# A planned attention-and-MoE kernel: loads cut into smaller pieces that are issued at landings, and new constants in its planner

## The chip, the cores and the metric

The kernel runs on one core of one Trainium2 chip. The metric is device time in microseconds of one execution. Engines are named as in the profile: PE (matrix multiply), PEld (its weight loads), DVE, ACT, POOL and SP; POOL issues the input loads and SP the output stores.

## The reference

Sliding-window attention over 8 batches, 8 heads, 576 positions, head size 64; then a soft mixture of experts on its output. Heads 0 to 3 see the last 32 positions, heads 4 to 7 every fourth of the last 128.

```python
scores = scale * q @ k.T                     # per batch and head
mask_plain = (rel >= 0) & (rel < 32)
mask_dil   = (rel >= 0) & (rel < 128) & (rel % 4 == 0)
attn = softmax(where(mask, scores, -1e9));  x = attn @ v      # x: 4608 x 512
logits = x @ phi                             # 32 slots, 4 per expert
d = softmax over tokens;  slot_input = d.T @ x
h = relu(slot_input[e] @ w1[e]);  slot_out[e] = h @ w2[e]     # 8 experts, F = 1024
c = softmax over slots;  out = c @ slot_out  # 4608 x 512, f32
```

Inputs are f32: q, k and v of 9.4 MB each, w1 and w2 of 16.8 MB each. The output is 9.4 MB.

## The kernel before, in words

**A program of ops and a planner.** The kernel doesn't write instructions in their final order. `P.op` (L123) records an op: which engines could run it and for how long by the author's estimate (`pe(t)`, `act(n)`, `dve(n)`, `dve2(n)`, L304 to L317), which buffers it reads and writes, which PSUM banks it needs, how many matmuls it has (`mm`), and, for a load, its bytes and semaphore. `schedule` (L162) then simulates the ops by these durations and takes, again and again, the op that could start first, with priority among those that start within `SLACK` of it. The result is a fixed order of instructions for each engine, and for ops that DVE or ACT could run the choice of the engine. `emit` (L238) writes that order with the semaphore waits that each op needs. On the chip the engines run their orders as given: an op that isn't ready holds up all behind it on its engine.

**The work.** 16 units, one for each batch and half of the heads. A unit has these stages: `stage_T` (L615) transposes K, Q and V from staging slots (L623 for an even unit, 18 matmuls each; L626 for an odd one, 9 each); `stage_V` (L639, matmuls L655) lays V out in 18 blocks; `stage_S` (L670) adds mask and scores in PSUM (L678, L681, and 72 small matmuls at L687); `stage_P` (L697) takes the maximum on DVE (L706, L708), subtracts it by matmul (L715), takes the exponential on ACT (L721) and transposes (L728); `stage_O` (L737) multiplies by V in 72 small matmuls (L749) and normalises on DVE (L759, L761); `stage_X` (L765) transposes the result (L779). After each second unit `gating` (L793) does the logits (L803), the running softmax over tokens, transposes (L836 to L853) and the sum into the slots (L870 to L880); after each fourth `combine` (L892) prepares the softmax over slots (L899 to L924). After the last unit come the experts: w1 at L1024, transposes L1044, w2 at L1058, of which the last two groups are expert 7's chunks 0 to 5 and 6 to 7. Then 36 matmuls (L1082) with copies (L1090, L1091), and 18 stores of 512 KB (L1095).

**The loads.** All are DMAs that POOL issues, casting f32 to bf16. `load` (L467, issue at L477) brings K, Q or V of a unit as one DMA into one of 9 staging slots, three units ahead; an even unit's has 256 rows of 1,152 bytes at the destination, an odd unit's 128 rows of 2,304. A slot can be loaded again only after the transposes that read it. `load_w` (L480, issue at L492) brings an expert's w1 or w2 in two DMAs of 64 partitions each (expert 7's w2 in chunks 0 to 5 and 6 to 7). Stage loads have priority 100n-100 and weights 1700, so that in the plan a weight load goes only where no stage load can. The last two experts' w2 lie in staging slots.

**What paces a load.** All but the first unit's loads are `paced`. Before, the planner lets a paced load start no earlier than 2.5 us (`DMA_LEAD` + `DMA_WAIT`) before its model of the DMA queue is free, 400 bytes a nanosecond. On the chip this becomes a wait for the op of PE, DVE, ACT or SP whose planned end lies last before the load's planned start:

```python
            if o.paced:
                near = [d for d in done_at[-60:] if d.end <= st]
                if near:
                    o.raw = o.raw | {max(near, key=lambda d: d.end)}
```

**The planner's model of instruction blocks.** It counts the matmuls given to PE. An op that would carry the count over `BLOCK` (127) may not start before a time that is `SUPPLY` (3.2 us), less half of the op, after the start of the op at which the count went over last:

```python
                if o.opts[0][0] == "PE" and n_mm + o.mm > self.BLOCK:
                    t0 = max(t0, blk_t + self.SUPPLY - 0.5 * o.opts[0][1])
```

The delay exists in the plan only; no wait on the chip comes from it. Its effect is the order.

Of the kernel before, what the change touches and what calls it, by code (L numbers as in the profile page):

```python
# [13 lines left out]
DM = H * D  # L14
E_EXP = 8
N_SLOTS = 32
FF = 1024
SCALE = 1.0 / (D ** 0.5)
NSU = 16
LSEQ = 2 * S  # L20
# [88 lines left out]
class Prog:  # L109
    LAT = dict(PE=0.28, DVE=0.08, ACT=0.08, POOL=0.1, SP=0.1)  # L110
    SLACK = 0.12
    DVE_MORE = 0.5
    BLOCK = 127
    SUPPLY = 3.2
    DMA_LEAD = 2.2
    DMA_WAIT = 0.3

    def __init__(self):
        self.ops = []
# [42 lines left out]
    def schedule(self):  # L162
        free = dict(PE=0.0, DVE=0.0, ACT=0.0, POOL=0.0, SP=0.0)
        dma_free = 0.0
        n_mm, blk_t = 0, 0.0
        done_at = []
        for o in self.ops:
            o.users = []
        for o in self.ops:
            o.nleft = 0  # L170
            for d in o.raw | o.war:
                d.users.append(o)
                o.nleft += 1
        done = lambda d: d.end + (0.0 if d.bytes else self.LAT[d.eng])
        ready = []

        def arm(o):
            o.start = max([done(d) for d in o.raw | o.war], default=0.0)
            ready.append(o)
        for o in self.ops:  # L180
            if o.nleft == 0:
                arm(o)
        order = []
        while ready:
            cands = []
            for o in ready:
                t0 = o.start
                bank = None
                if o.rounds and o.rounds[0].first is None:
                    rd = o.rounds[0]  # L190
                    bank = rd.pool.choose(rd.n, t0, done)
                    if bank is None:
                        continue
                    t0 = max(t0, bank[0])

                if o.paced:
                    t0 = max(t0, dma_free - self.DMA_LEAD - self.DMA_WAIT)

                if o.opts[0][0] == "PE" and n_mm + o.mm > self.BLOCK:
                    t0 = max(t0, blk_t + self.SUPPLY - 0.5 * o.opts[0][1])  # L200
                e, c = min(o.opts, key=lambda ec: max(t0, free[ec[0]]) + ec[1] +
                           (o.more if ec[0] == "DVE" else 0.0))
                cands.append((max(t0, free[e]), o.prio, o.idx, o, e, c, bank))
            assert cands, "no schedule"
            first = min(cands, key=lambda x: x[:3])
            same = [x for x in cands if x[4] == first[4] and x[0] <= first[0] + self.SLACK]
            st, _, _, o, e, c, bank = min(same, key=lambda x: (x[1], x[2]))
            if bank is not None:
                rd = o.rounds[0]
                rd.first = bank[1]  # L210
                for i in range(rd.n):
                    rd.pool.banks[bank[1] + i].round = rd
                o.war = o.war | (set(bank[2]) - o.raw)
            o.eng, o.start, o.end = e, st, st + c
            free[e] = st + c
            if e == "PE":
                n_mm += o.mm
                if n_mm > self.BLOCK:
                    n_mm, blk_t = n_mm - self.BLOCK, st
            if o.paced:  # L220
                near = [d for d in done_at[-60:] if d.end <= st]
                if near:
                    o.raw = o.raw | {max(near, key=lambda d: d.end)}
            if not o.bytes and e != "POOL":
                done_at.append(o)
            if o.bytes:
                dma_free = max(dma_free, o.end + 1.5) + o.bytes / 400e3
                o.end = dma_free + 0.5
            order.append(o)
            ready.remove(o)  # L230
            for u in o.users:
                u.nleft -= 1
                if u.nleft == 0:
# [82 lines left out]
def pe(t):  # L316
    return [("PE", t)]  # L317
# [12 lines left out]
def bass_dilated_sliding_attn__then__soft_moe_slots_kernel(  # L330
# [11 lines left out]
    P = Prog()  # L342
# [5 lines left out]
    NSLOT = 9  # L348
# [5 lines left out]
    slots = [stg_all[:, SLOT * i:SLOT * (i + 1)] for i in range(NSLOT)]  # L354
# [30 lines left out]
    mm = sb("mm", [128, B + 1, 2], F32)  # L385
# [37 lines left out]
    b_stg = [Buf() for _ in range(NSLOT)]  # L423
# [23 lines left out]
    s_stg = [nc.alloc_semaphore(f"s_stg{i}") for i in range(NSLOT)]  # L447
    s_w1 = [nc.alloc_semaphore(f"s_w1_{e}") for e in range(E_EXP)]
    s_w2 = [nc.alloc_semaphore(f"s_w2_{e}") for e in range(E_EXP)]
    s_w2l = [s_w2[E_EXP - 1], nc.alloc_semaphore("s_w2_last")]  # L450
# [16 lines left out]
    def load(w):  # L467
        n, t = w // 3, w % 3
        b, ty = su_bt(n)
        i = w % NSLOT  # L470
        hs = (k, q, v)[t][b, 4 * ty:4 * ty + 4]
        if ty == 0:
            dst = slots[i].rearrange("p (h c) -> p h c", h=2)
            ap = hs.rearrange("(p x) (i c) d -> (x i) p (c d)", p=2, c=9)
        else:
            dst, ap = slots[i], hs.rearrange("h (i c) d -> (h i) (c d)", c=18)
        P.op(POOL, lambda g: g.dma_start(dst, ap),  # L477
             w=[b_stg[i]], dma=(128 * LSEQ * 5, s_stg[i]), paced=n > 0)

    def load_w(kk, e):  # L480
        src, c, dst, b_w, sem = ((moe_w1, 4, w1b[:, e], b_w1[e], s_w1[e]) if kk == "1" else
                                 (moe_w2, 8, w2v[e], b_w2[e], s_w2[e]))
        ap = src[e].rearrange("(p c) f -> p c f", c=c)
        for i in range(2):
            if kk == "2" and e == E_EXP - 1:

                sl = (slice(0, 128), slice(0, 6) if i == 0 else slice(6, 8))
                size, bw, sem = DM * FF * (3 - 2 * i), b_w2l[i], s_w2l[i]
            else:
                sl = (slice(64 * i, 64 * i + 64), slice(0, c))  # L490
                size, bw = DM * FF * 2, b_w
            P.op(POOL, lambda g, sl=sl: g.dma_start(dst[sl], ap[sl]), paced=True,  # L492
                 dma=(size, sem), **(dict(w=[bw]) if i == 0 or bw is not b_w else dict(a=[bw])))


    P.cur = -1000
# [118 lines left out]
    def stage_T(n):  # L615
        u = n % 2
# [11 lines left out]
        for t in range(3):  # L628
            rd = Round(ring, 2)
            i = (3 * n + t) % NSLOT  # L630
            o = P.op(pe(0.47), lambda pe_, rd=rd, i=i: trs(pe_, rd, slots[i]),
                     r=[b_stg[i], b_ident], rounds=[rd], mm=18 - 9 * u)
            o.war |= set(b_seq[u][t].w + b_seq[u][t].r)
            dv = seq[u][:, t, PAD:PAD + LSEQ].rearrange("p (m c) -> p m c", c=9)
            P.op([act(1152), dve(1152)], lambda eng, dv=dv, rd=rd: cp(
                eng, dv, rd.h[:, 0:1152].rearrange("p (c m) -> p m c", m=128)),
                rounds=[rd], w=[b_seq[u][t]])

    def stage_V(n):  # L639
# [8 lines left out]
        for gi, part in enumerate((todo[:16], todo[16:])):  # L648
# [7 lines left out]
                                            seq[u][:, 2, sl], ident[:])  # L656
                return ins
            nt = sum(len(w) for w in part)
            o = P.op(pe(0.055 * nt), tr, r=[b_seq[u][2], b_ident], rounds=[rd], mm=nt)
            if gi == 0:  # L660
                o.war |= set(b_VOV[u].w + b_VOV[u].r)
            n_el = 128 * len(part)
# [7 lines left out]
    def stage_S(n):  # L670
# [3 lines left out]
        for p, t0, nt in ((0, 0, 10), (1, 10, 8)):  # L674
            rd = Round(ring, 2 - p)

            def fS(pe_, p=p, t0=t0, nt=nt, rd=rd):
# [6 lines left out]
                for p_ in range(2):  # L684
# [4 lines left out]
                                qk(u, p_, k, j, 1, 32, 0), qk(u, p_, k, j, 0, 64, 1),  # L689
                                start=False, stop=True, skip_group_check=True)  # L690
                return ins
            P.op(pe(0.06 * nt), fS, mm=4 * nt + 2 - p, rounds=[rd],
                 r=rr + [b_mask[u], b_mb, b_ident])
            res.append((rd, t0, nt))
        return res
# [1 line left out]
    def stage_P(n, rds):  # L697
        u = n % 2
        for i, (rd, t0, nt) in enumerate(rds):
# [11 lines left out]
            def sub(pe_, rd=rd, nt=nt, hi=hi, lo=lo):  # L711
                for a, b in ((0, 8), (8, nt)):
# [3 lines left out]
                                             m[:, a:b].unsqueeze(2).to_broadcast([128, b - a, 64]),  # L716
                                             start=False, stop=True, skip_group_check=True)
                return ins
            P.op(pe(0.08 + 0.0006 * ne), sub, r=[b_nm[u][i], b_nl[u][i], b_idneg],
                 rounds=[rd], mm=4 - 2 * i)  # L720
            P.op([act(ne)], lambda ac, t0=t0, rd=rd, ne=ne: ac.activation(  # L721
                pb[u][:, 64 * t0:64 * t0 + ne], rd.f[:, 0:ne], ACTF.Exp, scale=SCALE),
# [2 lines left out]
        for i, (a, b) in enumerate(((0, 5), (5, 9))):  # L725
            def tr(pe_, a=a, b=b):
# [1 line left out]
                    ins = pe_.transpose(rd.h[:, 128 * t:128 * t + 128],  # L728
                                        pb[u][:, 128 * t:128 * t + 128], ident[:])
                return ins  # L730
            o = P.op(pe(0.05 * (b - a)), tr, r=[b_pb[u][i], b_ident], rounds=[rd], mm=b - a)
# [5 lines left out]
    def stage_O(n):  # L737
        u = n % 2
        x = n % NX
        for p in range(2):  # L740
# [5 lines left out]
            def fO(pe_, p=p, rd=rd):  # L746
# [46 lines left out]
    def gating(b):  # L793
# [6 lines left out]
        def fL(pe_):  # L800
# [6 lines left out]
        P.op(pe(0.4), fL, r=[b_phi, b_xt[xs[0]], b_xt[xs[1]]], rounds=[rl], mm=16)  # L807
# [47 lines left out]
        P.op(pe(0.25), fD1, r=[b_dT, b_dT2, b_ident], rounds=[rd], mm=5)  # L855
        P.op(pe(0.15), fD2, r=[b_dT, b_dT2, b_ident], rounds=[rd], mm=5, hard=[o0])
# [4 lines left out]
        def fSl(pe_):  # L861
# [3 lines left out]
            for ty in range(2):  # L865
# [7 lines left out]
                if ty == 0:  # L873
# [8 lines left out]
        P.op(pe(0.7), fSl, r=[b_dn, b_xn[xs[0]], b_xn[xs[1]]], rounds=[rs], mm=20)  # L882
        if b == B - 1:
            return rs
        P.op([("DVE", 0.75)], lambda vv: vv.scalar_tensor_tensor(
# [255 lines left out]
```

## Time and profile before

| what | us |
|---|---|
| three runs | 245.57, 247.24, 251.96 (median 247.24) |
| the profiled execution: its time | 246.26 |
| its span, first to last instruction | 244.5 |
| PE, PEld busy | 186.6, 127.9 |
| DVE, ACT, POOL busy | 144.9, 122.8, 53.2 |
| packets of the loads (queue q0), share of 16 engines' span | 74.7% |
| last load lands, from the span's start | 213.9 |
| last w2 matmul group ends, first output matmul starts | 217.1, 217.8 |

Lines of the profile name an engine, a source line, an operation, the tile written and the tile read. `[2.73 <-issue]` behind an instruction means that its engine stood idle 2.73 us before it and that no semaphore event ended this; any other name there is the op that ended the wait. The chain is the run of work that ended last, followed back from the end. The clock is the share of TensorE's full clock that was granted. Besides these views the trace has a record for each DMA packet: queue, start, duration and bytes.

### The profile page before, as it was taken

How to read it: one execution, taken by the hardware profiler on the slowest of the kernel's cores; microseconds unless marked ns; L12 is line 12 of the kernel's file. 1: busy time of each engine (PE TensorE's matmuls, PEld its weight loads, DVE VectorE, ACT ScalarE, POOL GpSimd, SP SyncE). 2: the span in 40 equal slices, each digit the busy share in tenths (PEclk: the TensorE clock that was granted, in tenths of full speed). 3: DMA queues.
4: the chain of work that ended last, by engine and by line, in shares of the span. 5: the costliest groups of instructions: out<-in, count | busy, mean ns of one | idle time of the engine just before them, and what ended most of it. 6: DMA issues, size and time to landing. Idle time of an engine off the chain costs nothing.

```text
span 244.5 us, 9798 instructions
## 1 busy us (share of the span) xinstructions
PE 186.6 (76%) x4502; PEld 127.9 (52%) x4502; DVE 144.9 (59%) x319; ACT 122.8 (50%) x190; POOL 53.2 (22%) x113
## 2 busy tenths in 40 slices
PE   0896959897987869897989777996688586987410
PEld 0585746675665557663767555765466352542100
DVE  4145456557778766863788655768277556627440
ACT  2546835576747727673656644765444320135440
POOL 6545321312312222320223111111011210000000
PEclk9999997889999999996799997999797855999955
DMA  6979794979899997797799998699689999609998
GB/s 84 147 121 137 118 163 78 132 119 155 142 185 153 162 172 136 126 159 144 127 160 137 191 154 155 127 181 174 127 150 176 201 182 167 127 5 406 401 407 328
DMA packets 15881, 41.06 MB, mean 168 GB/s; under 512 B 2144, under 2 KB 8288, under 8 KB 13920
## 3 DMA queue, kind: packets, MB, share of 16 engines
q0 software_dynamic: 12672, 30.94, 74.7%
q1 hardware_dynamic: 3168, 9.50, 10.0%
q8 instruction: 35, 0.57, 0.9%
q14 instruction: 6, 0.05, 0.1%
HBM read 61.93 MB, written 9.44 MB: 292 GB/s over the span
## 4 chain that ended last, share of the span: by engine, by line
PE 64%; DVE 11%; issue 10%; DMA 7%; ACT 4%; POOL 0%; DVEq 0%; POOLq 0%
PE ps L655 7%; PE ps L715 7%; PE ps L687 6%; PE ps L623 6%; PE ps L626 5%; DMA out_dram<-aren 5%; PE ps L728 4%; PE ps L779 4%; PE ps L678 3%; PE ps L749 3%; DVE aren L327 3%; DMA stg_all<-in_v_dram 3%; DVE xn L761 2%; PE ps L1082 2%; PE ps L1058 2%
## 5 line engine op out<-in xcount | busy, mean ns | idle before, releaser
L326 ACT ACTIVATE aren<-ps 128x1152 bf16<-128x1152 bf16 (+2 forms) x48 | 53.5, 1130 | 38.2 <-PE ps L655 17.8
L327 DVE COPY aren<-ps 128x1152 bf16<-128x1152 bf16 (+2 forms) x32 | 33.5, 1053 | 15.3 <-PE ps L655 6.4
L706 DVE TENSOR_REDUCE nm<-ps 128x10 f32<-128x640 f32 (+1 forms) x32 | 24.1, 754 | 14.8 <-PE ps L687 14.8
L687 PE MATMUL ps<-aren 64*32 64x64 bf16 x1152 | 17.3, 194 | 16.5 <-issue 16.5
L687 PEld LDWEIGHTS ps<-aren 64*32 64x32 bf16 x1152 | 12.0, 94 | 26.4 <-issue 26.4
L326 ACT ACTIVATE xt<-ps 128x640 bf16<-128x640 bf16 (+1 forms) x20 | 12.7, 659 | 25.5 <-PE ps L779 25.5
L761 DVE TENSOR_TENSOR xn<-ps,rv 128x576 bf16<-128x576 f32 x32 | 24.2, 758 | 1.1
L655 PE MATMUL ps<-ident,aren 128*128 128x128 bf16 (+1 forms) x304 | 23.5, 236 | 1.2 <-issue 0.5
L721 ACT ACTIVATE pp<-ps 128x640 bf16<-128x640 f32 (+1 forms) x32 | 20.4, 652 | 6.1 <-PE ps L715 5.4
L623 PE MATMUL ps<-ident,stg_all 128*64 128x128 bf16 x432 | 17.7, 235 | 7.0 <-DMA stg_all<-in_k_dram 6.2
L655 PEld LDWEIGHTS ps<-ident,aren 128*128 128x128 bf16 (+1 forms) x304 | 18.6, 107 | 3.4 <-issue 1.0
L623 PEld LDWEIGHTS ps<-ident,stg_all 128*64 128x64 bf16 x432 | 14.1, 119 | 10.7 <-POOL mbase L510 6.2
L1091 DVE COPY aren<-ps 128x512 f32<-128x512 f32 x18 | 11.9, 688 | 11.4 <-PE ps L1082 6.6
L626 PE MATMUL ps<-ident,stg_all 128*128 128x128 bf16 x216 | 18.1, 238 | 0.7 <-DVE aren L327 0.7
L715 PE MATMUL ps<-nm,idneg 128*128 128x512 bf16 (+1 forms) x48 | 16.9, 359 | 0.6 <-DVE nl L708 0.4
L749 PE MATMUL ps<-aren,pp 64*32 64x65 bf16 x1152 | 14.2, 195 | 3.7 <-issue 1.5
L492 POOL DMA_DIRECT2D w1b<-in_moe_w_dram x16 | 8.5, 529 | 38.1 <-PE ps L749 9.0
L626 PEld LDWEIGHTS ps<-ident,stg_all 128*128 128x128 bf16 x216 | 15.1, 108 | 3.0 <-DVE aren L327 0.9
L477 POOL DMA_DIRECT2D stg_all<-in_k_dram x16 | 10.3, 644 | 26.4 <-DVE nl L708 4.4
L715 PE MATMUL ps<-nl,idneg 128*128 128x512 bf16 (+1 forms) x48 | 15.4, 355 | 0.0
L728 PE MATMUL ps<-ident,pp 128*128 128x128 bf16 x144 | 13.8, 230 | 2.0 <-DVE nl L708 1.3
L477 POOL DMA_DIRECT2D stg_all<-in_v_dram x16 | 9.9, 619 | 23.3 <-DVE nl L708 4.6
(143 smaller groups left out, 302.8 us busy)
## 6 DMA issues: line engine op xcount, KB each, us to landing
out_dram<-aren SPq DMA_DIRECT2D x18, 512.0 KB, 5.5
w1b<-in_moe_w_dram POOLq DMA_DIRECT2D x16, 512.0 KB, 7.1
w2b<-in_moe_w_dram POOLq DMA_DIRECT2D x12, 512.0 KB, 7.2
stg_all<-in_k_dram POOLq DMA_DIRECT2D x16, 288.0 KB, 5.3
stg_all<-in_q_dram POOLq DMA_DIRECT2D x16, 288.0 KB, 5.3
stg_all<-in_v_dram POOLq DMA_DIRECT2D x16, 288.0 KB, 5.1
stg_all<-in_moe_w_dram POOLq DMA_DIRECT2D x2, 512.0 KB, 7.3
stg_all<-in_moe_w_dram POOLq DMA_DIRECT2D x1, 768.0 KB, 8.5
```

Source lines behind the costliest of these rows:

```text
L326: return eng.activation(dst, src, ACTF.Copy)
L327: return eng.tensor_copy(dst, src)
L623: ins = pe_.transpose(rd.h[64 * p:64 * p + 64, oc], sl[:, 576 * p + 64 * c:576 * p + 64 * c + 64], ident[:])
L626: ins = pe_.transpose(rd.h[:, oc], sl[:, oc], ident[:])
L655: ins = pe_.transpose(rd.h[row:row + nk, 128 * i:128 * i + 128], seq[u][:, 2, sl], ident[:])
L687: ins = pe_.matmul(rd.f[32 * j:32 * j + 32, 64 * (tile - t0):64 * (tile - t0) + 64], qk(u, p_, k, j, 1, 32, 0), qk(u, p_, k, j, 0, 64, 1), ...
L706: P.op([dve(ne)], lambda vv, sv=sv, nv=nv: vv.tensor_reduce(nv, sv(), AXX, AluOp.max), rounds=[rd], w=[b_nm[u][i]])
L715: ins = pe_.matmul(rd.f[:, 64 * a:64 * b], idneg[:], m[:, a:b].unsqueeze(2).to_broadcast([128, b - a, 64]), start=False, stop=True, skip_g ...
L721: P.op([act(ne)], lambda ac, t0=t0, rd=rd, ne=ne: ac.activation(pb[u][:, 64 * t0:64 * t0 + ne], rd.f[:, 0:ne], ACTF.Exp, scale=SCALE), rou ...
L728: ins = pe_.transpose(rd.h[:, 128 * t:128 * t + 128], pb[u][:, 128 * t:128 * t + 128], ident[:])
L749: ins = pe_.matmul(rd.f[32 * oq:32 * oq + 32, 103 * pl:103 * pl + 65], pt[u][sl, tile // 2, 32 * j:32 * j + 32], VOV[u][sl, pv, j % 2 if u ...
L761: P.op([dve(576)], lambda vv, cols=cols, rvp=rvp, p=p: vv.tensor_tensor(xn[x][:, :, p, :], cols(0, 64), rvp.unsqueeze(2).to_broadcast([128 ...
```

## The change

It does four things.

1. A stage load becomes two DMAs of 64 partitions each, and a weight load four of 32 (expert 7's w2: four of two chunks each), every one with a semaphore of its own. A reader waits for all pieces that it reads. 80 issues become 160.
2. A paced load no longer waits for a compute op. It waits for the landing of an earlier load: going back from the last load issued, the planner adds up planned transfer times (bytes over 400 a nanosecond) until they reach `COVER` (1.8 us), and takes the load before those. Its landing is the earliest start in the plan, and a wait on its semaphore on the chip.
3. The block model starts with the count at `BLOCK` - `FIRST` (127.3 - 94), so its places are 94, 221.3, 348.6 and so on in place of 127, 254, 381; `SUPPLY` is 3.4; the time of a place is taken inside the op, in proportion to its matmuls.
4. The estimated durations of 11 PE ops change, nearly all upwards. The planned latency of a DMA goes from 1.5 + 0.5 to 1.3 + 0.4 us around its transfer.

The operations, their operands and the buffers stay the same. The order on each engine, and which of DVE and ACT runs an op that either could, are the planner's result and can change everywhere.

```diff
-    BLOCK = 127
-    SUPPLY = 3.2
-    DMA_LEAD = 2.2
-    DMA_WAIT = 0.3
+    BLOCK = 127.3
+    FIRST = 94
+    SUPPLY = 3.4
+    COVER = 1.8
...
-        n_mm, blk_t = 0, 0.0
-        done_at = []
+        n_mm, blk_t = self.BLOCK - self.FIRST, 0.0
+        loads = []
+        clk = None
...
         while ready:
+
+            clk, under = None, 0.0
+            for d, c in reversed(loads):
+                if under >= self.COVER:
+                    clk = d
+                    break
+                under += c
...
-                if o.paced:
-                    t0 = max(t0, dma_free - self.DMA_LEAD - self.DMA_WAIT)
+                if o.paced and clk is not None:
+                    t0 = max(t0, clk.end)
 
                 if o.opts[0][0] == "PE" and n_mm + o.mm > self.BLOCK:
-                    t0 = max(t0, blk_t + self.SUPPLY - 0.5 * o.opts[0][1])
+
+                    t0 = max(t0, blk_t + self.SUPPLY - o.opts[0][1] * (self.BLOCK - n_mm) / o.mm)
...
                 n_mm += o.mm
                 if n_mm > self.BLOCK:
-                    n_mm, blk_t = n_mm - self.BLOCK, st
-            if o.paced:
-                near = [d for d in done_at[-60:] if d.end <= st]
-                if near:
-                    o.raw = o.raw | {max(near, key=lambda d: d.end)}
-            if not o.bytes and e != "POOL":
-                done_at.append(o)
+                    n_mm -= self.BLOCK
+                    blk_t = st + c * (1 - n_mm / o.mm)
+            if o.paced and clk is not None:
+                o.raw = o.raw | {clk}
             if o.bytes:
-                dma_free = max(dma_free, o.end + 1.5) + o.bytes / 400e3
-                o.end = dma_free + 0.5
+                dma_free = max(dma_free, o.end + 1.3) + o.bytes / 400e3
+                o.end = dma_free + 0.4
+                if e == "POOL":
+                    loads.append((o, o.bytes / 400e3))
...
+    NPQ, NPW = 2, 4
...
-        P.op(POOL, lambda g: g.dma_start(dst, ap),
-             w=[b_stg[i]], dma=(128 * LSEQ * 5, s_stg[i]), paced=n > 0)
+        m = 128 // NPQ
+        for j in range(NPQ):
+            sl = slice(m * j, m * j + m)
+            P.op(POOL, lambda g, sl=sl: g.dma_start(dst[sl], ap[sl]),
+                 dma=(m * LSEQ * 5, s_stg[i][j]), paced=n > 0,
+                 **(dict(w=[b_stg[i]]) if j == 0 else dict(a=[b_stg[i]])))
...
-        for i in range(2):
+        m = 128 // NPW
+        for i in range(NPW):
...
-                size, bw, sem = DM * FF * (3 - 2 * i), b_w2l[i], s_w2l[i]
+                r = 8 // NPW
+                sl = (slice(0, 128), slice(r * i, r * i + r))
+                bw = b_w2l[i // (NPW - 1)]
...
-                sl = (slice(64 * i, 64 * i + 64), slice(0, c))
+                sl = (slice(m * i, m * i + m), slice(0, c))
...
             P.op(POOL, lambda g, sl=sl: g.dma_start(dst[sl], ap[sl]), paced=True,
+                 dma=(4 * DM * FF // NPW, sem[i]),
...
-            o = P.op(pe(0.47), lambda pe_, rd=rd, i=i: trs(pe_, rd, slots[i]),
+            o = P.op(pe(0.5 if u else 0.62), lambda pe_, rd=rd, i=i: trs(pe_, rd, slots[i]),
...
-            o = P.op(pe(0.055 * nt), tr, r=[b_seq[u][2], b_ident], rounds=[rd], mm=nt)
+            o = P.op(pe(0.03 + 0.055 * nt), tr, r=[b_seq[u][2], b_ident], rounds=[rd], mm=nt)
...
-            P.op(pe(0.06 * nt), fS, mm=4 * nt + 2 - p, rounds=[rd],
+            P.op(pe(0.22 + 0.056 * nt), fS, mm=4 * nt + 2 - p, rounds=[rd],
...
-            P.op(pe(0.08 + 0.0006 * ne), sub, r=[b_nm[u][i], b_nl[u][i], b_idneg],
+            P.op(pe(0.15 + 0.0006 * ne), sub, r=[b_nm[u][i], b_nl[u][i], b_idneg],
...
-            P.op(pe(0.32), fO, r=[b_pt[u], b_VOV[u]], rounds=[rd], mm=36)
+            P.op(pe(0.38), fO, r=[b_pt[u], b_VOV[u]], rounds=[rd], mm=36)
...
-        o0 = P.op(pe(0.3), fD0, r=[b_dT, b_ident], rounds=[rd], mm=10)
+        o0 = P.op(pe(0.6), fD0, r=[b_dT, b_ident], rounds=[rd], mm=10)
```

Left out are the other changed estimates: the transposes of L728 (0.05 to 0.06 a matmul), the logits (0.4 to 0.45), two more groups of gating transposes (0.25 to 0.34, 0.15 to 0.27) and the sum into the slots (0.7 to 0.67).

More of the change, by code (lines that the diff above doesn't have):

```diff
@@ L446, in bass_dilated_sliding_attn__then__soft_moe_slots_kernel @@
     b_w2l = [b_w2[E_EXP - 1], Buf()]
[L447 to L450, printed above, removed]
+    NPQ, NPW = 2, 4
+    s_stg = [[nc.alloc_semaphore(f"s_stg{i}_{j}") for j in range(NPQ)] for i in range(NSLOT)]
+    s_w1 = [[nc.alloc_semaphore(f"s_w1_{e}_{j}") for j in range(NPW)] for e in range(E_EXP)]
+    s_w2 = [[nc.alloc_semaphore(f"s_w2_{e}_{j}") for j in range(NPW)] for e in range(E_EXP)]
     s_phi = [nc.alloc_semaphore(f"s_phi{i}") for i in range(4)]
@@ L483, in load_w @@
         ap = src[e].rearrange("(p c) f -> p c f", c=c)
-        for i in range(2):
+        m = 128 // NPW
+        for i in range(NPW):
             if kk == "2" and e == E_EXP - 1:
-                sl = (slice(0, 128), slice(0, 6) if i == 0 else slice(6, 8))
-                size, bw, sem = DM * FF * (3 - 2 * i), b_w2l[i], s_w2l[i]
-            else:
-                sl = (slice(64 * i, 64 * i + 64), slice(0, c))
-                size, bw = DM * FF * 2, b_w
+                r = 8 // NPW
+                sl = (slice(0, 128), slice(r * i, r * i + r))
+                bw = b_w2l[i // (NPW - 1)]
+            else:
+                sl = (slice(m * i, m * i + m), slice(0, c))
+                bw = b_w
             P.op(POOL, lambda g, sl=sl: g.dma_start(dst[sl], ap[sl]), paced=True,
-                 dma=(size, sem), **(dict(w=[bw]) if i == 0 or bw is not b_w else dict(a=[bw])))
+                 dma=(4 * DM * FF // NPW, sem[i]),
+                 **(dict(w=[bw]) if i == 0 or bw is b_w2l[1] else dict(a=[bw])))
     P.cur = -1000
@@ L730, in tr @@
                 return ins
-            o = P.op(pe(0.05 * (b - a)), tr, r=[b_pb[u][i], b_ident], rounds=[rd], mm=b - a)
+            o = P.op(pe(0.06 * (b - a)), tr, r=[b_pb[u][i], b_ident], rounds=[rd], mm=b - a)
             if i == 0:
@@ L806, in fL @@
             return ins
-        P.op(pe(0.4), fL, r=[b_phi, b_xt[xs[0]], b_xt[xs[1]]], rounds=[rl], mm=16)
+        P.op(pe(0.45), fL, r=[b_phi, b_xt[xs[0]], b_xt[xs[1]]], rounds=[rl], mm=16)
         P.op([dve(192)], lambda vv: vv.tensor_reduce(
@@ L853, in fD2 @@
             return pe_.transpose(o(576, 608)[0:64], dT[96:128, 192:256], i4)
-        o0 = P.op(pe(0.3), fD0, r=[b_dT, b_ident], rounds=[rd], mm=10)
-        P.op(pe(0.25), fD1, r=[b_dT, b_dT2, b_ident], rounds=[rd], mm=5)
-        P.op(pe(0.15), fD2, r=[b_dT, b_dT2, b_ident], rounds=[rd], mm=5, hard=[o0])
+        o0 = P.op(pe(0.6), fD0, r=[b_dT, b_ident], rounds=[rd], mm=10)
+        P.op(pe(0.34), fD1, r=[b_dT, b_dT2, b_ident], rounds=[rd], mm=5)
+        P.op(pe(0.27), fD2, r=[b_dT, b_dT2, b_ident], rounds=[rd], mm=5, hard=[o0])
         P.op([dve2(608), act(608)], lambda eng: cp(
@@ L881, in fSl @@
                               skip_group_check=True)
-        P.op(pe(0.7), fSl, r=[b_dn, b_xn[xs[0]], b_xn[xs[1]]], rounds=[rs], mm=20)
+        P.op(pe(0.67), fSl, r=[b_dn, b_xn[xs[0]], b_xn[xs[1]]], rounds=[rs], mm=20)
         if b == B - 1:
```

## The prediction

> **What bounds the kernel now.** I read first the page's busy shares and chain, then the busy time of the attention stretch alone, then PE's waits in it, then the places of those waits, then the loads.
>
> ```profile
> PE 186.6 (76%) x4502; PEld 127.9 (52%) x4502; DVE 144.9 (59%) x319; ACT 122.8 (50%) x190; POOL 53.2 (22%) x113
> ...
> PE 64%; DVE 11%; issue 10%; DMA 7%; ACT 4%; POOL 0%; DVEq 0%; POOLq 0%
> ```
>
> ```profile
> 9.30:186.00 176.70, 149.54 (x4033) 108.84 (x4034) 112.95 (x235) 102.19 (x154) 43.44 (x86) 0.94 0.87 147
> ```
>
> ```profile
> PE ps L687 <- issue: 16.5, 11, 3.6
> PE ps L840 <- issue: 2.0, 1, 2.0
> PE ps L749 <- issue: 1.5, 1, 1.5
> PE ps L728 <- DVE nl L708: 1.3, 1, 1.3
> ```
>
> From 9.3 to 186 us (the columns: stretch, PE, PEld, DVE, ACT, POOL busy, clock, DMA) PE is busy 149.5 of 176.7 us; DVE and ACT have a third of it free. PE's 27.2 us of idle time are 20.7 of "issue" (16.5 + 2.0 + 1.5 + 0.5 + 0.2 in the list of waits) and some 6.5 of true dependencies. "Issue" is the thing to explain:
>
> ```profile
> 32.77 0.41 PE L687 MATMUL ps<-aren 64*32 64x64 bf16 x28
> ...
> 35.90 0.23 PE L687 MATMUL ps<-aren 64*32 64x64 bf16 x4 [2.73 <-issue]
> ```
>
> ```profile
> q0 software_dynamic: 12672, 30.94, 74.7%
> ...
> q8 instruction: 35, 0.57, 0.9%
> ```
>
> The gap sits in the middle of one op. Counting matmuls in the trace, gaps begin at the 350th, 604th, 859th, 1113th, 1241st, 1368th, and so on to the 4041st: every 127.3, (4041-350)/29. The trace's packet records have 35 instruction packets of 16 KB, one after each such place. At 30.16 PE crosses a place; the packet starts at 33.58, takes 0.95, and PE, which by 32.96 has run out of instructions at the next place, goes on at 35.90, 1.37 after the packet's end. Over 34 crossings the wait from crossing to packet start is 2.57 on average (0.5 to 4.5), the packet about 0.95, the restart about 1.4: a supply of 4.9 us a block. The dense blocks of QK and PV matmuls need only 2.3 to 2.9 us (22.66-19.78, 32.96-30.16, 169.42-167.08), so they stall. The wait follows the loads in flight: 1.22 at 119.26 and 1.09 at 156.64 with one load outstanding, 4.50 at 160.16 with three and 3.82 at 167.08 with two weight halves.
>
> ```profile
> w2b<-in_moe_w_dram POOLq DMA_DIRECT2D x12, 512.0 KB, 7.2
> stg_all<-in_k_dram POOLq DMA_DIRECT2D x16, 288.0 KB, 5.3
> ```
>
> These are issue-to-landing times under load. Nearly alone a stage load takes 3.47 to 3.99 (issued at 51.33, 41.62, 17.63), a weight half 5.19 to 5.28; one behind another they land every 1.4 to 1.7 and 2.4 to 2.5. So the fixed part is about 2.2 and 2.75 us. The last load lands at 213.94, and the last MoE block starts near then: loads and compute end together.
>
> **Part 1, the wait for instructions.** Before, two to three whole loads lie in flight (some 1.6 or 2.5 us of transfer each); after, the COVER rule lets a piece go when two pieces (0.92 + 0.92 or more in planned time, so always two) are behind the one that landed: three pieces of 0.8 or 1.25 us. I scale the part of the wait above the quiet 1.1: 2.57 - 1.1 = 1.47, times about 0.42 for smaller and fewer queued bytes, gives 0.6; the wait is 1.7, 0.85 less. The 18 stalls of PEld at block places before 186 are 2.08, 2.94, 0.73, 1.33, 0.44, 1.60, 1.18, 2.26, 1.13, 0.36, 1.74, 0.79, 1.33, 1.91, 1.52, 0.64, 3.87, 0.46, together 26.3. Less 0.85 each, not below zero, 12.7 are left, 48%. On PE's own 20.7 that is -10.7. Ends: 0 (a stream that never pauses keeps the wait as it is) to -20.7; I take the middle because the quiet rows (1.1 to 1.2) show the wait does fall, and a block of 2.3 to 2.9 still stalls at 1.7 + 0.95 + 1.4 = 4.05.
>
> **Part 2, block places.** The old planner's places are 127, 254...; the real ones 94, 221...: 33 matmuls off, so its spacing acted on the wrong ops. The new ones agree with the gaps within 2 matmuls in this program. The new program has an extra semaphore wait at most stage loads (two pieces, two semaphores; 51 ns each on PE's sequencer, hidden under matmuls of 235 ns): some 25 to 50 instructions over 9,062 move the places by up to 20 matmuls at the end, which I cost at a smaller gain. A gain of 2, between +3 (worse mixes) and -5.
>
> **Part 3, PE durations and order.** The planned op costs rise towards the rows (18 K transposes 0.47 to 0.62, measured 0.62; PV 0.32 to 0.38). They change the static order on PE, DVE and ACT. The 6.5 us of dependencies were partly hidden behind the stalls, since DVE and ACT catch up while PE stands; with half of the stalls gone I add 3.5, between 0 and 10.7 (all of what Part 1 gave).
>
> **Part 4, the clock.** PEclk is half speed in windows that follow stalls: 37.2 to 40.6 after the 2.9 us one, 112.3 to 119.2, 173.8 to 177.2 after the 3.87. A V-transposing group of nine takes 0.90 at 37.28 and 0.50 at 29.26, a set of nine X transposes 0.96 and 0.61, so a 3.4 us window costs about 1.1; seven such windows lie between 37 and 187.5 (7.7 us). I take two away: -2.2 (0 to -7.7).
>
> Compute side: -10.7 - 2 + 3.5 - 2.2 = -11.4.
>
> **Part 5, the load stream.** 80 issues become 160. POOL takes 0.515 (64 rows), 0.53 to 0.56 (128 rows) or 0.70 to 0.72 (256 pieces) an issue, so 80 more cost POOL about 42 us over 200 in which it is busy 53: hidden, as long as an issue (0.5) is shorter than the spacing (1.0). What is new is the wait at the head of POOL's queue: every later load, and early the affine selects, stand behind it, and PE's transposes stand behind those. With three in flight a piece takes a third of its loop: stage (2.2 + 0.8)/3 = 1.0, weights (2.75 + 1.25 + 0.05)/3 = 1.35. The first six land by 9.3 as now; 90 x 1.0 + 64 x 1.35 = 176. About 31 instruction packets put 0.95 on one engine each, of which 0.6 is not caught up: 19. The stream ends near 9.3 + 176 + 19 = 204, against 213.9 now; q0's packets alone fill 74.7% of 244.5 = 183 us of all engines, so about 187 is the floor. After the last landing there are two matmuls and the tail from 217.15 on, 27.6: a span of 232. Stage loads come first in the plan, so the late ones are weights.
>
> **Two rules weighed.** The trace shows 20.7 us of PE idle at block places. The Trainium skill, "Runtime: NRT & Kernel Launch", Instruction fetch mechanics, says that crossing a 16 KiB block costs one tail-bump, mostly hidden; by it Parts 1 and 2 would be about 0 and the sum would be +1.3. The trace disagrees, so the trace stands. Against the change speaks "DMA: Bandwidth & Descriptors", Rules for kernel authors: two transfers to disjoint partition halves bring no bandwidth, use one. By it the stream would end where it does now, 213.9, and the sum would be about 0. The trace of before has no half piece of a stage load, so it can't say yet.
>
> **Prologue.** Three stage loads issue in 2.3 us, six half ones in some 3.3: the identity's select moves from 3.72 to about 4.7, covered until the first transposes at 6.16; the mask's selects end near 8.0 against 8.96 for their reader. V's landing at 9.27 is set by transfers. 0, or +1 without that cover.
>
> **Sum.** The profiled execution took 246.26 (span 244.5 plus 1.8). Compute gives 246.26 - 11.4 = 234.9, the stream 232 + 1.8 = 234; the later of two uncertain ends is about a microsecond above either, and the median of the runs shown (247.24) stands 1.0 above the profiled one: **236**.
>
> **The rivals.**
> - *Stalls turn into waits* (0.21): the supply hardly falls, or DVE and ACT hand PE the same time back. For: dependencies are 6.5 only because stalls cover them. Against: DVE and ACT are 64% and 58% busy. Time 246 +-3.
> - *The stream of small pieces is the bound, and slower* (0.16): three pieces don't cover a loop if a half piece takes nearly a whole one's 3.95 and 5.25. At the worst 90 x 1.32 + 64 x 1.75 = 231, the stream ends at 240 even without instruction packets, and the time is 240 + 27.6 + 1.8 = 269. It decides from an end at 223 on (252): a mean spacing, packets included, of (223 - 9.3)/154 = 1.39 against my 1.27. Against: a half piece has half the transfer, 0.8 or 1.25 us less of the latency, and nothing in the rows makes up for that. Typical time 257.
> - *Stalls nearly gone* (0.08): the planner mixes dense and sparse ops into blocks of 4 us. Floor 246.3 - 20.7 - 7.7 = 218; typical 226.
> - My forecast, both ends earlier (0.55): 229 to 243.
>
> **Chances.** About 5 us either way (2%) is what a measurement of this kernel can tell from no change. Faster (below 242.3): 0.08 + 0.52 of the forecast + 0.02 of the first rival = 0.62. Within 2%: 0.19 + 0.03 + 0.01 = 0.23. Slower: 0.15. The range leaves out most of the slower rival and the floor: 228 to 252.
>
> **What would show it.** Right: instruction packets start about 1.7 us after a crossing; PE's issue waits from 9 to 186 fall to near 8 to 10; the last weight lands by 207; POOL waits on landings, not on PE and DVE ops. Wrong: gaps stay at 127-matmul places with the same wait (Part 1); PE waits on ACT and DVE grow beyond 12 (Part 3); POOL's spacing is over 1.4 a piece and the last MoE block waits for a DMA (Part 5); PE's transposes wait for stage loads.

## The result, and the profile after

The changed kernel takes 276.99 us (median of 4 runs, 274.76 to 279.04) against 249.60 (245.57 to 255.27) for the kernel before in the same comparison: a ratio of 1.121, 95% interval 1.100 to 1.143. It is slower by 12%, 41 us above the forecast and 25 above the range. Executions of one kernel differ by a few per cent, at different granted clocks: a ratio here compares only those within 1.5% of their kernel's fastest, a median takes in all. The profiled execution took 274.76, its span is 273.0.

The page of the changed kernel has the chain that ended last, two rows of its busy tenths (40 slices of 6.8 us), and the row of the w2 matmuls (busy time, mean ns, idle time of PE before them and what ended it):

```profile
DMA 47%; PE 32%; issue 7%; ACT 5%; DVE 5%; POOL 2%; POOLq 0%; DVEq 0%; ACTq 0%
```

```profile
PE   1788899898999896898982897579000413567530
...
PEclk9999999999999999999997799757755555559755
```

```profile
L1073 PE MATMUL ps<-w2b,pp 128*32 128x512 bf16 x48 | 7.2, 630 | 34.1 <-DMA w2b<-in_moe_w_dram 34.1
```

Before, 64% of the chain was PE's work and 7% DMA. Now 47% is DMA, and the PE row is nearly empty in slices 29 to 34 (191 to 232 us): the attention is done and the experts wait 34.1 us for weights. The clock row shows the cost that comes with it, half speed (5) in these slices.

Two things happened at once. Attention became much faster. The first w1 matmul starts at 183.51, where it was 204.58. These are the stretches from 9.3 us to the experts (stretch, PE, PEld, DVE, ACT, POOL busy, clock, DMA share, GB/s) of the kernel after and then of the kernel before:

```profile
9.30:183.90 174.60, 147.21 (x4224) 109.95 (x4254) 120.41 (x260) 108.67 (x170) 67.79 (x141) 0.95 0.83 126
```

```profile
9.30:204.50 195.20, 161.49 (x4246) 116.13 (x4246) 124.40 (x267) 108.34 (x168) 46.91 (x93) 0.91 0.88 150
```

And PE's waits in the stretch after:

```profile
PE ps L641 <- DMA stg_all<-in_k_dram: 6.3, 1, 6.3
PE ps L702 <- issue: 3.8, 7, 1.5
PE ps L794 <- DVE xn L776: 2.4, 4, 1.7
PE ps L764 <- issue: 2.3, 3, 1.5
...
PE ps L696 <- issue: 1.2, 6, 0.3
```

"Issue" has fallen from 20.7 us to 7.3 (3.8 + 2.3 + 1.2). The instruction packets start 1.22 us after PE crosses a block place, on average over 34 crossings; before it was 2.57. PE's busy time is 14 us less, but not all of that is real: the trace lacks 27 of 4,502 matmul records, 26 of them mask matmuls of L693 (0.38 us each), and the 1.2 us at L696 stand just behind such missing rows. The run with more in flight only for w2, below, has the same plan up to the last 32 loads and lacks no record; there PE is busy for 152.6 us up to the experts, 9 less than before. The half-clock time falls by enough for that: there are 16.8 us at half clock between 16.5 us and the experts, where there were 34.2. The first wait of the list is new, 6.3 us for a stage load: the stream of loads is late.

The stream is the second thing. The last load lands at 243.39; before it was 213.94. The waits of POOL show that its queue now stands for landings:

```profile
POOL w2b L506 <- DMA w2b<-in_moe_w_dram: 25.8, 21, 2.0
POOL w1b L506 <- DMA w1b<-in_moe_w_dram: 24.9, 15, 3.6
POOL stg_all L488 <- DMA stg_all<-in_k_dram: 16.4, 17, 2.1
```

The DMA issues (count, KB each, median us from issue to landing) show what a piece takes when three are in flight:

```profile
w1b<-in_moe_w_dram POOLq DMA_DIRECT2D x32, 256.0 KB, 5.0
stg_all<-in_k_dram POOLq DMA_DIRECT2D x32, 144.0 KB, 3.5
```

The means over all paced pieces are 5.07 for weights and 3.59 for stage loads. The chain in order of time (start, duration, what) gives the loop itself:

```profile
194.60 4.91 DMA w2b<-in_moe_w_dram
199.52 0.28 issue
199.80 4.59 DMA w2b<-in_moe_w_dram
204.38 0.28 issue
204.66 4.98 DMA w2b<-in_moe_w_dram
209.64 0.28 issue
```

A piece lands, 0.28 us later POOL issues the piece that waited for it, and that one lands 4.6 to 5.0 us on. Three such chains run side by side, so a quarter of a weight matrix comes in each 1.7 us. Its transfer alone is about 1.25, the median time between landings of weight pieces in the run with COVER 4.0 below, where five are in flight.

The stream's lateness is paid for a second time. The w2 matmuls after and before (minimum, median, maximum in ns):

```profile
L1073 PE MATMUL ps<-w2b,pp x48: 583/634/634, 215.4 to 232.4; 128*32 128x512 bf16 x48
```

```profile
L1058 PE MATMUL ps<-w2b,pp x48: 379/379/390, 211.4 to 215.0; 128*32 128x512 bf16 x48
```

PE stood idle from 191.2 us on, and from 193.97 the granted clock was half, for 51.2 us, over the waits and the matmuls between them. From the last landing to the end of the span it took 29.6 us (273.0 - 243.39) where I had 27.6.

### The profile page after: what moved, and what is told of

Read it like the earlier page. It is cut to its first block, busy times and chain, and to the rows that moved or that the text cites. A ratio compares the mean times of both kernels' runs of the same rounds, so it can differ in the third digit from the quotient of the medians.

```text
span 273.0 us, 9911 instructions
## 1 busy us (share of the span) xinstructions
PE 182.6 (67%) x4475; PEld 123.8 (45%) x4502; DVE 141.5 (52%) x317; ACT 122.7 (45%) x192; POOL 90.3 (33%) x193
## 4 chain that ended last, share of the span: by engine, by line
DMA 47%; PE 32%; issue 7%; ACT 5%; DVE 5%; POOL 2%; POOLq 0%; DVEq 0%; ACTq 0%
DMA w2b<-in_moe_w_dram 14%; DMA w1b<-in_moe_w_dram 13%; DMA stg_all<-in_v_dram 6%; DMA stg_all<-in_moe_w_dram 6%; PE ps L670 5%; DMA out_dram<-aren 4%; PE ps L702 4%; ACT aren L333 4%; PE ps L730 3%; DMA stg_all<-in_k_dram 3%; DVE aren L334 3%; PE ps L638 3%; PE ps L641 2%; PE ps L764 2%; PE ps L1097 2%
## 5 line engine op out<-in xcount | busy, mean ns | idle before, releaser
L333 ACT ACTIVATE aren<-ps 128x1152 bf16<-128x1152 bf16 (+2 forms) x53 | 57.0, 1088 | 41.2 <-PE ps L670 17.5
L334 DVE COPY aren<-ps 128x1152 bf16<-128x1152 bf16 (+2 forms) x27 | 28.9, 1074 | 11.7 <-PE ps L670 4.6
L1073 PE MATMUL ps<-w2b,pp 128*32 128x512 bf16 x48 | 7.2, 630 | 34.1 <-DMA w2b<-in_moe_w_dram 34.1
L506 POOL DMA_DIRECT2D w1b<-in_moe_w_dram x32 | 15.8, 494 | 36.5 <-DMA w1b<-in_moe_w_dram 24.9
L488 POOL DMA_DIRECT2D stg_all<-in_k_dram x32 | 17.9, 560 | 28.1 <-DMA w1b<-in_moe_w_dram 8.0
L488 POOL DMA_DIRECT2D stg_all<-in_v_dram x32 | 17.5, 549 | 21.7 <-DMA stg_all<-in_k_dram 11.2
L488 POOL DMA_DIRECT2D stg_all<-in_q_dram x32 | 17.5, 549 | 19.4 <-DMA stg_all<-in_k_dram 5.2
L641 PE MATMUL ps<-ident,stg_all 128*128 128x128 bf16 x216 | 16.8, 226 | 8.2 <-DMA stg_all<-in_k_dram 6.3
L506 POOL DMA_DIRECT2D w2b<-in_moe_w_dram x24 | 11.7, 490 | 29.9 <-DMA w2b<-in_moe_w_dram 25.8
L1073 PEld LDWEIGHTS ps<-w2b,pp 128*32 128x32 bf16 x48 | 2.3, 138 | 37.6 <-issue 27.4
L641 PEld LDWEIGHTS ps<-ident,stg_all 128*128 128x128 bf16 x216 | 13.2, 101 | 11.3 <-DMA stg_all<-in_k_dram 6.5
```

Of the source, the lines that this page charges most:

```text
L333: return eng.activation(dst, src, ACTF.Copy)
L334: return eng.tensor_copy(dst, src)
L488: P.op(POOL, lambda g, sl=sl: g.dma_start(dst[sl], ap[sl]), dma=(m * LSEQ * 5, s_stg[i][j]), paced=n > 0, **(dict(w=[b_stg[i]]) if j == 0 ...
L641: ins = pe_.transpose(rd.h[:, oc], sl[:, oc], ident[:])
```

## The experiments

Two theories to begin with. *A: too few pieces in flight.* COVER 1.8 leaves two pieces behind the one that landed; three in flight share a loop of some 5.3 us for weights and 3.9 for stage loads, and that bounds the stream. *B: small pieces are slow in themselves* (more DMAs, more waits, whatever is in flight). A third was kept open, *C: the order that the planner found is to blame*.

**More in flight, with the same pieces.** Two kernels with one number changed; the first is shown, the second has 4.0 in its place:

```diff
-    COVER = 1.8
+    COVER = 2.7
```

> COVER 2.7 in place of 1.8: three pieces behind the one that landed, so four in flight in place of three; all else as changed. Theory A (too few pieces in flight: after the change one piece takes 0.28 us from landing to issue and about 5.0 to its own landing, three share that, 1.67 to 1.75 us a weight piece): four share it, the spacing falls to about 1.4 (stage about 0.95), the last load lands near 200 in place of 243, the time is 225 to 240. Theory B (small pieces are slow by themselves, whatever is in flight): last landing stays past 230, time 262 or more. Theory C (the planner's new order is to blame): 262 or more.

> COVER 4.0: five stage pieces or four weight pieces behind, five or six in flight. Theory A: the stream is then limited by the transfers (weights 1.25 to 1.4 a piece) and ends near 195 to 200; the wait of the instruction packets, 1.22 us after the change, rises to 2 or more, and PE's issue waits with it; time 228 to 242, not below the run with COVER 2.7. Theory B: 262 or more.

Measured: COVER 2.7 gives 239.0 us, ratio to before 0.961 (0.945 to 0.977), last landing 209.15; COVER 4.0 gives 245.8, ratio 0.989 (0.959 to 1.018), last landing 193.16. With the same 160 pieces the stream ends 34 and 50 us earlier, so B falls. C doesn't fall by these two alone, since each COVER gives an order of its own; the run with the loads alone, below, has another order and the same slow stream. COVER 2.7 lands later than expected (209 against 200), and 245.8 lies above the range for COVER 4.0. Between pieces of one kind lie 1.30 us (stage) and 1.77 (weights) at COVER 1.8, 1.12 and 1.49 at 2.7, 1.02 and 1.34 at 4.0. The price is on the other side: the packet's wait goes from 1.22 to 1.98 and 2.29, the first w1 matmul from 183.5 to 195.1 and 201.8 (the starts of the experts in the expectations are read at a later matmul of the same group). Of the waits of PE in the run with 4.0:

```profile
PE ps L702 <- issue: 8.9, 6, 2.2
...
PE ps L764 <- issue: 4.4, 3, 3.6
...
PE ps L818 <- issue: 2.7, 1, 2.7
```

Of the three, the time is least at 2.7, between the end that the stream sets and the end that the stalls set.

**The plan alone.** The kernel before with its whole loads and its pacing, and the changed block model and all 11 PE durations, of which only the model is shown:

```diff
-    BLOCK = 127
-    SUPPLY = 3.2
+    BLOCK = 127.3
+    FIRST = 94
+    SUPPLY = 3.4
...
+                    blk_t = st + c * (1 - n_mm / o.mm)
...
```

> The kernel before with the new block places, SUPPLY and PE durations, but its own whole loads, paced by compute ops. If the new plan is what made attention end earlier after the change (experts start at 184 in place of 204.6): the experts start by 195, time 230 to 240. If the shorter wait of the instruction packets did it: the wait stays near 2.5 us, the experts start after 200, time 242 to 252. Theory C (order to blame): 255 or more.

Measured: 253.9 us (249.2 to 254.9) beside 252.4 (246.9 to 257.4) for the kernel before; no gain, in the quickest executions either (249.2 against 246.9). The packet's wait is 2.55, the first w1 matmul starts at 207.74, and "issue" is as large as before:

```profile
PE ps L689 <- issue: 12.3, 9, 3.1
PE ps L625 <- issue: 3.5, 1, 3.5
PE ps L751 <- issue: 2.5, 3, 1.5
...
PE ps L848 <- issue: 1.4, 1, 1.4
...
PE ps L876 <- issue: 0.9, 1, 0.9
```

That is 20.6 us in rows over 0.8 alone. The wait and the late experts are as the second expectation has them; the time lies above its 252. Block places within a few matmuls of the true ones changed which op stalls, not how much.

**The loads alone.** The changed loads under the old plan, its old durations included (not shown):

```diff
-    BLOCK = 127.3
-    FIRST = 94
-    SUPPLY = 3.4
+    BLOCK = 127
+    FIRST = 127
+    SUPPLY = 3.2
...
```

> The changed loads (small pieces, issued at landings, COVER 1.8, new DMA latencies in the plan) with the old block places and PE durations. Theory A: the stream is as slow as after the whole change, last landing 235 to 250, time 266 to 282. Theory C: back to 255 or less.

Measured: 275.8 us, ratio 1.109 (1.096 to 1.123), last landing 243.08, first w1 matmul 182.94, packet's wait 1.38. Both effects of the change, the faster attention and the slow stream, are here whole, without its plan:

```profile
DMA 60%; PE 22%; issue 6%; ACT 5%; DVE 2%; POOL 2%; SPq 0%; POOLq 0%; DVEq 0%; ACTq 0%
```

**More in flight only when attention is over.** The last 32 pieces are w2's, and they are issued after 185 us.

```diff
-                if under >= self.COVER:
+                if under >= (self.COVER if len(loads) < 128 else 4.0):
```

> As changed (COVER 1.8), but the last 32 pieces, w2's, which are issued after attention has ended, go with COVER 4.0 (five in flight). If the wait for the landing with too few in flight is what the time is lost to: their spacing falls from 1.67 to about 1.3, the last load lands 12 us earlier, near 231, the time falls by as much, to 260 to 266; attention and the start of the experts stay as after the change (184). If the transfers themselves are slow then: no change, 272 to 278.

Measured: 258.2 us, ratio 1.028 (1.025 to 1.032); last landing 228.03, 15 us earlier than after the change; first w1 matmul 180.8. The time lies just below the expected span, with the mechanism as A has it: between the landings of these 32 pieces lie 1.25 us, where it was 1.75 after the change. The chain shows the longer loop, now shared by five:

```profile
195.68 5.94 DMA w2b<-in_moe_w_dram
201.61 0.28 issue
201.89 5.82 DMA w2b<-in_moe_w_dram
207.71 0.28 issue
```

**Fewer in flight.** One execution, to see why three pieces take 3.59 and 5.07 us on average when the quickest take 2.85 and 3.77:

```diff
-    COVER = 1.8
+    COVER = 0.9
```

> COVER 0.9: one piece behind, two in flight; all else as changed. After the change a stage piece takes 3.59 us from issue to landing on average and a weight piece 5.07, the quickest 2.85 and 3.77. If the difference is queueing of the three pieces behind one another: with two the means fall to about 3.1 and 4.2, spacing (0.28 + 3.1)/2 = 1.7 and (0.28 + 4.2)/2 = 2.2, last landing near 300, time about 330. If small pieces are intrinsically that slow: means stay at 3.6 and 5.1, spacing 1.9 and 2.7, last landing about 350, time about 380.

Measured: 353.1 us, last landing 321.82, between the two expectations. The means fall to 3.32 and 4.38. So 0.27 and 0.69 us of the latency at three in flight come from the third piece. At two in flight 0.5 to 0.6 over the quickest is left. The spacing is the loop shared by two: (0.28 + 3.32)/2 = 1.80 and (0.28 + 4.38)/2 = 2.33, measured 1.80 and 2.33. Whether that is the second piece, the instruction packets or the slowest of the 16 engines (first and last engine land 0.75 and 1.31 us apart here) was not tried.

**Whole loads, issued at landings.**

```diff
-    NPQ, NPW = 2, 4
+    NPQ, NPW = 1, 2
...
-                r = 8 // NPW
-                sl = (slice(0, 128), slice(r * i, r * i + r))
+                sl = (slice(0, 128), slice(0, 6) if i == 0 else slice(6, 8))
```

> Whole stage loads and weight halves as before, but issued at landings with COVER 1.8, which leaves two in flight (as many bytes as four pieces). If bytes in flight set both the stream and the instruction packets' wait: like COVER 2.7, last landing 205 to 218, packet wait 2.0, time 237 to 247. If the size of a piece sets the packets' wait: wait 2.4 or more, experts start after 202, time 245 to 255. If whole loads are free of the loss between pieces: last landing below 203.

Measured: 260.5 us, ratio 1.035 (1.029 to 1.041), last landing 232.51, packet's wait 1.64, first w1 matmul 190.4 (the profiled execution took 262.5, 2 over the median). None of the expectations had it: as many bytes in flight as with COVER 2.7, and yet a slower stream (2.70 us a stage load and 3.22 a weight half, against 2 x 1.12 and 2 x 1.49) and a shorter wait. The loop gives it: a whole stage load took 4.85 us and a weight half 6.24, so (0.28 + 4.85)/2 = 2.57 and (0.28 + 6.24)/2 = 3.26. Two wholes keep the DMA engines less filled than four halves (0.81 busy from 9.3 to 186 us, against 0.94). So at equal bytes in flight the size of a piece matters, and for the stream in favour of small ones. The Trainium skill, "DMA: Bandwidth & Descriptors", Rules for kernel authors, says not to bother with two transfers to disjoint partition halves. With the old pacing that agrees with the next run, 246.0 us for halves against 248.3 for wholes. Where the issue hangs on landings it doesn't: halves gave 239.0 us (0.961 of the kernel before) and wholes 260.5 (1.035).

**Half pieces, paced by compute ops as before.**

```diff
-                if o.paced and clk is not None:
-                    t0 = max(t0, clk.end)
+                if o.paced:
+                    t0 = max(t0, dma_free - self.DMA_LEAD - self.DMA_WAIT)
...
-            if o.paced and clk is not None:
-                o.raw = o.raw | {clk}
+            if o.paced:
+                near = [d for d in done_at[-60:] if d.end <= st]
+                if near:
+                    o.raw = o.raw | {max(near, key=lambda d: d.end)}
```

> Half and quarter pieces and the new plan, but paced as before: each load waits for a compute op, at the planner's old DMA times. If the waiting for landings is what slows the stream: without it the last load lands by 216, time 238 to 254. If cutting loads slows the stream: last landing past 230, time 262 or more. The packets' wait: if the size of pieces sets it, below 1.7 us; if what is in flight does, 2.2 or more as before.

Measured: 246.0 us, ratio 0.985 (0.965 to 1.005), last landing 211.39, packet's wait 2.29, first w1 matmul 204.27. Cutting alone neither slows the stream nor shortens the packet's wait: with 4.8 pieces in flight on average at the issue of a stage piece (4.2 at a weight's) it is the kernel before again.

**Between 2.7 and 4.0, and the old plan at 2.7.** The first has this edit; the second is the kernel with the loads alone, with 2.7 in place of 1.8.

```diff
-    COVER = 1.8
+    COVER = 3.6
```

> COVER 3.6: four stage pieces or three weight pieces behind, five or four in flight, between the runs with 2.7 (239.0, last landing 209.15, experts start at 195.97) and 4.0 (245.8, 193.16, 202.67). If in-flight pieces trade the stream against the instruction packets: last landing about 203, experts start about 198 to 200, time 238 to 243. If the order that each plan happens to give matters more than that: anywhere from 232 to 252.

> The changed loads with COVER 2.7 and the old block places and PE durations, against the same with the new ones (239.0 us, experts start at 195.97). If the new places and durations are worth anything where the stream isn't the bound: 242 to 250, experts start at 199 or later. If they are worth nothing: 236 to 242.

COVER 3.6: the four times spread from 239.6 to 250.4, median 248.2, too far for a verdict against 239.0 or 245.8. The profiled execution is the quickest of them: last landing 200.63, first w1 matmul 196.8, packet's wait 2.28. The old plan at 2.7: 240.6 (234.1 to 243.4), first w1 matmul 200.8 in a profiled execution of 243.4. That is not told apart from 239.0 either; the plan's worth is at most a few us where the stream is not the bound, and none was shown.

**The best of it.** COVER 2.7, and 4.0 for w2, beside COVER 2.7 once more:

```diff
-    COVER = 1.8
+    COVER = 2.7
...
-                if under >= self.COVER:
+                if under >= (self.COVER if len(loads) < 128 else 4.0):
```

> COVER 2.7, and 4.0 for the last 32 pieces (w2). If the stream still ended last with 2.7 (last landing 209.15, last w2 group near 210.5): last landing near 200 to 204, time 233 to 238. If the compute side is level with it already: experts start at 196 and need 13 us to the end of the w2 groups, so no gain beyond 1 us, 237 to 241.

> COVER 2.7 once more, beside the two runs built on it, on their chip: 237 to 243, faster than the kernel before by 3 to 5%.

Measured: 234.0 us (233.6 to 234.9), ratio to before 0.946 (0.939 to 0.954); COVER 2.7 again 239.0, ratio 0.964 (0.953 to 0.976). The first beats both kernels (0.946 of the kernel before, where the changed one is 1.121), and lies where the first of its two expectations had it. Its chain after attention has compute and no load:

```profile
191.18 5.93 PE ps L1039 x61
197.12 0.63 PE ps L1059 x8
...
200.91 3.49 PE ps L1073 x32
...
205.32 5.18 PE ps L1097 x21
```

Its w2 matmuls run at full clock again (379 ns), and the last load lands at 203.29, before its matmuls are reached.

## Why the prediction was wrong

**What bounds the kernel now: right.** "Issue" is the wait of PE for instruction packets behind load packets, one at each 127.3 matmuls. The runs bear it out: with small pieces under the new plan the packet's wait moves with what is in flight (1.02 with two, 1.22 with three, 1.98 with four, 2.29 with five or so), and attention moves with the wait and with the half-clock time, as long as stage loads are on time (with two in flight they aren't).

**Part 1 (wait 1.7, -10.7): right in kind, too small.** The wait fell to 1.22, and "issue" on PE by 13.4. The kernel with the loads alone, with a wait of 1.38 and 4.7 us of "issue", shows that it comes from the loads.

**Part 2 (block places, -2) and Part 3 (order): not there.** The plan alone gave nothing. The 3.5 us that I added for dependencies that come to light didn't come either: up to the experts PE's waits for DVE went from 9.1 to 8.8 and those for ACT stayed at 2.9. What grew are waits for stage loads that came late, from 0.6 to 6.6.

**Part 4 (clock, -2.2): too small.** Half-clock time ahead of the experts went from 34.2 to 16.8 us. With the shorter waits this is why they start 21 us earlier against the 11.4 that I summed. That the shorter stalls brought it is not shown: in the other runs half-clock time goes from 18.5 to 51.7, and it was 18.5 both in the run with more in flight only for w2 (wait 1.6, experts from 180.8) and at COVER 3.6 (wait 2.28, experts from 196.8). So the waits alone are worth most of the 16 us between those two, and part of any one run's attention time is in its clock.

**Part 5 (the stream, end at 204): this is the step that failed.** "With three in flight a piece takes a third of its loop: stage (2.2 + 0.8)/3 = 1.0, weights (2.75 + 1.25 + 0.05)/3 = 1.35." The third is right; the loop is not. I took the latency of a piece that is alone (3.0 and 4.0; the quickest measured, 2.85 and 3.77, agree with it) for pieces that travel in threes. With three in flight a piece takes 3.59 and 5.07 on average. Of what lies over the quickest, 0.74 and 1.30, the third piece brings 0.27 and 0.69, as the run with two in flight shows; what brings the rest stays open. And from landing to issue it takes 0.28, of which I had 0.05 for the weights and nothing for the stage loads. So (0.28 + 3.59)/3 = 1.29 and (0.28 + 5.07)/3 = 1.78. Over 90 and 64 pieces that is 26 + 28 = 54 us, of which the 19 that I had set aside for instruction packets is a part: 204 + 54 - 19 = 239, measured 243.4. The error was in adding a quiet latency to a count of pieces in flight, while the same text had the loaded latency of whole pieces at hand (5.3 and 7.2 on the page against 3.5 to 4.0 and 5.2 alone).

**The rivals.** The slower rival had the mechanism, the place and, at its worst end, the spacings (1.32 and 1.75); its condition, that a half piece takes nearly a whole one's 3.95 and 5.25, is what was measured, 3.59 and 5.07. I gave it 0.16 with the argument that nothing makes up for the halved transfer; the latency under load did. Its typical price, 257, is from the middle of an interval, and the range's top, 252, from its near end, while its worst end (269) was the true case. The measured 277 lies above even that, by the late tail at half clock (+2), the stream's further 3 us and some 2 between executions. The prologue cost nothing, as predicted: the first stage loads land at 9.36 against 9.27.

**The profile's signs.** Of what I said would show me wrong, "POOL's spacing is over 1.4 a piece and the last MoE block waits for a DMA" is what the profile shows: 1.52 on average ((243.39 - 9.36)/154), and 34.1 us of PE waiting for w2.

## What to carry to other kernels

A transfer that is issued at the landing of an earlier one runs at pieces in flight over loop time, and the loop time is the loaded latency, with the step from landing to issue, never the quiet one. The division is bookkeeping and held within 5% at two and three in flight; the latency to put in has to be one at the depth that the rule will keep. Depth is a trade here: with fewer pieces in flight instruction packets start sooner and PE's stalls are shorter, more keep the weights on time, and the best depth is where both ends meet, which can differ by stage (deeper once PE has no dense stretch left). When a change sums a gain on one side and a bound on the other, the side with the thinner margin decides the range, however right the gain is.

## What the runs showed of the hardware

- From the landing of a DMA to the start of the POOL issue that waits for it: 0.28 us in 81% of the issues of the changed kernel. PE went on 0.04 after a landing in the kernel before (9.27, 9.31).
- Halving a load did not halve the time that POOL takes to issue it: mostly 0.49 us for 32 rows of a weight and 0.515 for 64, and 0.51 to 0.59 for a half stage load against 0.53 to 0.73 for a whole one.
- The instruction packet's wait for a given share of busy DMA engines does not follow the share: at 0.83 busy it was 1.22 us (three small pieces), at 0.94 it was 1.98 (four small ones), at 0.88 it was 2.57 (two to three large ones), at 0.81 it was 1.64 (two large ones).
- The Trainium skill, "Runtime: NRT & Kernel Launch", Instruction fetch mechanics, has the crossing of a block mostly hidden. In these runs it isn't: PE's "issue" stalls up to the experts were 20.7 us before and 7.3 after.
